# Attention and a gated feed-forward layer on one core: products of zeros between TensorE's early instructions, and a new order of the first two blocks

## The chip, the cores and the metric

The kernel runs on one core of one Trainium2 chip. The time is the device time of one execution in microseconds (us), of which the median of three runs is given. A profile comes from one further execution, whose own time is given beside it.

## The reference

Inputs are q, k, v of shape (4, 8, 768, 64), eight memory keys and values for each head, and the weights of a gated feed-forward layer with 512 inputs and 1536 hidden columns. All is in float32.

```python
for c in range(24):                       # chunks of 32 queries
    q_c   = q[:, :, 32*c : 32*c+32]
    k_ctx = k[:, :, max(0, 32*c-16) : min(768, 32*c+40)]      # 16 to the left, 8 to the right
    k_full = concatenate([mem_k, k_ctx]); v_full = concatenate([mem_v, v_ctx])
    a = softmax(q_c @ k_full.T / 8)
    attn[:, :, chunk] = a @ v_full
x  = attn as (3072 tokens, 512)
xn = x / sqrt(mean(x*x) + 1e-6) * rms_g
g  = xn @ w_gate
out = (g * sigmoid(g) * (xn @ w_val)) @ w_out
```

## The kernel before

The 3072 tokens are worked in eight blocks of 384. A block's attention is four units, each of two heads: unit 0 to 3 belong to block 0, 4 to 7 to block 1. The feed-forward layer goes over twelve slices of 128 hidden columns. Each product of the layer is split into three, of high and low parts, so one slice's gate (or value) is 12 matmuls of 384 columns, and its share of the output is 9 matmuls of 512 columns.

The first two blocks (all of their attention, and most of their feed-forward layer) are issued in the order of a written table, `ORDER`. A token is a letter (the step) and a number (the unit, or a place in the list of slices). Each step issues its instructions on whatever engines it uses, and each engine and each DMA queue works its own instructions strictly in the order of the table. The steps are:

- `U`, `V`: SyncE issues the loads of a unit's q and k, and of its v. `Z`: it issues the load of the next weight chunk.
- `S`: 24 small score matmuls (`s`). `M`, `a`: VectorE takes the row maximum and subtracts it. `E`: ScalarE takes the exponential. `d`, `n`: VectorE sums, inverts and scales.
- `P`: three transposes on TensorE (`pT`). `C`, `m`: ScalarE copies the two halves of the result to SBUF (`pt`). `O`: 12 matmuls with v (`o`).
- `Q`, `G`: ScalarE squares (`xq`), TensorE sums over partitions with a one-column operand (`ss`). `y`: VectorE and GpSimd make the inverse root of the mean. `Y`: TensorE spreads it over the partitions (`rb`, three matmuls). `z`: ScalarE copies it.
- `B`, `D`: ScalarE writes the high part (`xh`), VectorE the low part (`xl`) of the normalised input.
- `p`, `q`: a quarter (three matmuls) of the gate or value of the first slice (`pg`, `pv`). `g`, `v`: a whole gate or value (12 matmuls). `r`, `h`, `i`, `j`, `k`, `l`: what VectorE and ScalarE do on them. `o`: the output matmuls (`po`).
- `J`, `F`, `f`, `I`, `H`, `L`: the steps of ScalarE and VectorE that split a loaded weight chunk into its high and low part.

`p0` to `p3` and `q0` to `q3` are the first slice of block 0, `g1` and `v1` the first of block 1. `Y1` (the second `rb`) stands right behind `v1` in the table of both kernels, and behind it comes `o0`.

Scores, transposes and some other results share three PSUM buffers; gate and value have one bank each, so the next gate waits until VectorE's step `r` has read the last one. At the start, before the table, two matmuls of 512 columns are issued into a bank called `warm` (line 552). A step `W` exists (`warm`, line 187), but the table before has no such token. Behind the table the rest of the kernel (six blocks) is put in order by a scheduler.

Of the kernel before, what the change touches and what calls it, by code (L numbers as in the profile page):

```python
# [9 lines left out]
F32R = mybir.dt.float32r  # L10
# [8 lines left out]
B, H, S, D = 4, 8, 768, 64  # L19
# [5 lines left out]
P = 128  # L25
# [46 lines left out]


ORDER = """
U0 U1 U2 Z U3 S0 U4 M0 a0 U5 S1 M1 a1 V0 S2 E1 E0 M2 d0 J Z V1 U6 S3 a2 n0 E2 M3 P0 V2 F S4 Z C0a a3 m0a n1 E3
V3 f P1 d1 C1a V5 O0 m1a S5 Q0 V4 M4 J n2 U7 O1 a4 B0 n3 E4 G0 M5 B1 V7 I P2 Q1 S6 a5 C2a Z D0 m2a G1 H D1 P3
E5 M6 O2 m3a L C3a d2 O3 Q2 B2 p0 Q3 a6 B3 G2 n5 J G3 n4 F P5 y0 P4 m5a f p1 C5a D2 C4a S7 m4a I E6 O5 M7 Z H
D3 p2 V6 B5 a7 Y0 L E7 O4 d3 z0 Q5 q0 Q4 B4 p3 D5 J q1 n6 q2 n7 P6 D4 P7 f G4 m6a F G5 C6a r0 m7a F O6 C7a h0
I O7 Q6 i0 Z f q3 Q7 B7 G6 B6 D7 G7 J y1 D6 g1 j0 I k0a v1 H l0 Z H F L Y1 L o0 z1 r1 f h1 J g2 I i1 Z H r2 fa
g3 L j1 F v2 k1a l1 I h2 J o1 i2 Z j2 f H v3 r3 k2a F J L g4 l2 I h3 J o2 i3 Z j3 r4 F k3a v4 l3 f h4 fa g5 F  # L80
i4 I H o3 r5 Z j4 I k4a v5 Z H l4 L H g6 L h5 J i5 j5 o4 f J L v6 r6 k5a F J l5 f g7 I h6 fa i6 o5 Z r7 F j6 H
g8 F I k6a L Z H v7 l6 I h7 o6 i7 Z H j7 L k7a v8 J l7 r8 L o7 h8 J i8 f g9 j8 F k8a J I v9 r9 Z l8 f h9 o8 fa
F i9 j9 g10 F k9a I H l9 v10 Z H r10 L J I o9 h10 i10 Z f g11 j10 L k10a J l10 v11 F H r11 I h11 L Z J o10 Z
i11 j11 f k11a g12 H fa v12 J r12 l11 F J F F o11 L h12 I fa Z i12 j12 H g13 F k12a I fa L l12 J v13 I r13 Z H
I L H Z g14 h13 fa i13 L H o12 r14 j13 L k13a v14 J l13 F I h14 F o13 Z H J L F g15 i14 j14 f k14a I v15 r15 H
l14 f h15 J I R0 o14 i15 H L j15 g16 f k15a l15 L v16 r16 F h16 I i16 H o15 L j16
"""


# [1 line left out]
def tile_kernel(ctx: ExitStack, tc: tile.TileContext, q, k, v, w_gate, w_val, w_out, rms_g, out):  # L91
    nc = tc.nc
    const = ctx.enter_context(tc.tile_pool(name="const", bufs=1))
    p1 = ctx.enter_context(tc.tile_pool(name="p1", bufs=1))
    p2 = ctx.enter_context(tc.tile_pool(name="p2", bufs=2))
    p3 = ctx.enter_context(tc.tile_pool(name="p3", bufs=3))
# [37 lines left out]
    def psum_m(tag, name):  # L134
        return psm.tile([P, 512], F32, name=name, tag=tag)
# [49 lines left out]
        return nc.vector.tensor_copy(out=out, in_=in_)  # L185

    def warm(n):

        if ("part", "v", 0) in sp and len(pmw) == 1:
            pmw.append(psum_m("o0", "warm1"))  # L190
        w = pmw[-1]
        for _ in range(n):
            nc.tensor.matmul(w[0:64, 0:64], lhsT=zero, rhs=zero, start=True, stop=True)

    def stage_s(u):
        d = st[u]
# [81 lines left out]
    def stage_p(u, tag=None):  # L278
        d = st[u]
        t = psum_m(tag, f"pT{u}") if tag else psum_a(f"pT{u}")  # L280
        pe = d["p"].rearrange("p j k -> p (j k)")
        for i in range(NT):
            on_pe(nc.tensor.transpose(out=t[:, i * P:(i + 1) * P], in_=pe[:, i * P:(i + 1) * P], identity=ident))  # L283
        d["t"] = t
# [164 lines left out]
    def w_next(fn, *e):  # L449

        c = wpos[fn]
        wpos[fn] += 1
        fn(c, *e)
# [81 lines left out]
    pmw, sp = [], {}  # L535
    manual = tc.manual_schedule()
    manual.__enter__()
    zero = early.tile([P, 64], F32, name="zero", tag="zero")
# [157 lines left out]
    def tok_o(n):  # L696
# [5 lines left out]
    steps = dict(  # L702

        U=load_qk, V=load_v, Z=lambda n: w_load(), W=warm, R=tok_R,

        S=stage_s, M=stage_ma, a=stage_mb, E=stage_e, d=lambda k: stage_da(2 * k), n=stage_db,
        P=lambda n: stage_p(n, "o0" if n < NG else None),
# [7 lines left out]
        J=lambda n: w_next(w_open), F=lambda n: w_next(w_clamp), f=lambda n, *e: w_next(w_sign, *e),  # L715
        I=lambda n: w_next(w_shift),
        H=lambda n, *e: w_next(w_high, *e), L=lambda n, *e: w_next(w_low, *e))
# [638 lines left out]
```

## Time and profile before

| what | value |
|---|---|
| median of three runs | 666.61 us (665.45 to 666.87) |
| the profiled execution's own time | 671.41 us |
| its span, first to last instruction | 669.6 us |
| TensorE busy | 657.9 us (98%) |
| VectorE, ScalarE busy | 503.3 us, 334.7 us |
| mean granted TensorE clock | 0.987 of 2.4 GHz |

A granted clock of 1.00 is 2.4 GHz, 0.50 is 1.2 GHz. PE is TensorE's matmuls, PEld its weight loads, DVE is VectorE, ACT ScalarE, POOL GpSimd, SP the SyncE queue. A matmul's duration in a row holds its way through the array, so rows overlap; what one costs in a dense stretch is the distance from its start to the next start.

### The profile page before, as it was taken

To read this page: it belongs to the slowest core of one execution; us is meant where nothing else is said; L and a number is where in the kernel's file an instruction comes from. 1 tells how busy PE (TensorE), PEld (TensorE's weight loads), DVE (VectorE), ACT (ScalarE), POOL (GpSimd) and SP (SyncE) were. 2 spreads that over 40 slices of the span, in tenths; PEclk is the share of its full clock that TensorE was granted. 3 is DMA by queue.
4 is the path that set the end of the run, shared out by engine and by line. 5 is a ranking of instruction groups with operands and counts; after the bars stand their busy time and mean duration, and the time that the engine had idled before them with its cause. 6 is when DMAs were issued, how large, how long until landed. Compare 5 with 4: busy or idle time off the path is not lost.

```text
span 669.6 us, 15527 instructions
## 1 busy us (share of the span) xinstructions
PE 657.9 (98%) x6238; PEld 612.1 (91%) x6238; DVE 503.3 (75%) x1020; ACT 334.7 (50%) x642; POOL 4.7 (1%) x12
## 2 busy tenths in 40 slices
PE   6999999999999999999999999999999999999998
PEld 4898999999899999989999999999888899999997
DVE  6699999777688788877859567569638378888964
ACT  4779887843434435354445454345335233434553
POOL 0010000000000000000000000000000000000000
PEclk8699999999999999999999999999999999999999
DMA  9645454249698778345439779797643599987102
GB/s 324 251 159 181 185 189 146 106 135 351 187 374 302 254 247 291 107 168 165 143 126 369 262 235 308 253 294 256 191 142 116 170 352 331 320 303 265 52 9 71
DMA packets 82039, 145.46 MB, mean 217 GB/s; under 512 B 7472, under 2 KB 34608, under 8 KB 81968
## 3 DMA queue, kind: packets, MB, share of 16 engines
q1 hardware_dynamic: 80096, 141.32, 62.2%
q10 hardware_dynamic: 1872, 3.15, 1.4%
q8 instruction: 49, 0.80, 0.5%
q14 instruction: 22, 0.18, 0.1%
HBM read 109.84 MB, written 34.60 MB: 216 GB/s over the span
## 4 chain that ended last, share of the span: by engine, by line
PE 88%; DVE 4%; DMA 3%; ACT 2%; issue 1%; SPq 0%; DVEq 0%
PE pg L473 14%; PE po L523 14%; PE pv L473 13%; PE po L1195 8%; PE mva L949 7%; PE mga L949 7%; PE pa L1115 4%; PE mve L949 3%; PE mge L949 3%; PE pe L1115 2%; PE s L220 2%; PE oe L314 2%; PE mgc L949 2%; PE mvc L949 2%; PE pT L283 1%; DMA kv<-qp 1%
## 5 line engine op out<-in xcount | busy, mean ns | idle before, releaser
L473 PE MATMUL pg<-xh,wh_g 128*128 128x384 f32 x192 | 67.3, 351 | 0.7 <-DVE rg L482 0.7
L473 PE MATMUL pg<-xh,wl_g 128*128 128x384 f32 x192 | 65.3, 340 | 0.0
L473 PE MATMUL pg<-xl,wh_g 128*128 128x384 f32 x192 | 65.2, 340 | 0.0
L473 PE MATMUL pv<-xh,wh_v 128*128 128x384 f32 x192 | 65.2, 339 | 0.0
L473 PE MATMUL pv<-xl,wh_v 128*128 128x384 f32 x192 | 64.9, 338 | 0.0
L473 PE MATMUL pv<-xh,wl_v 128*128 128x384 f32 x192 | 64.8, 338 | 0.0
L949 PE MATMUL mva<-x,r 128*128 128x384 f32 x288 | 58.2, 337 | 0.1
L949 PE MATMUL mga<-x,r 128*128 128x384 f32 x288 | 58.2, 337 | 0.1
L523 PE MATMUL po<-wh_o,hh 128*128 128x512 f32 x141 | 56.7, 402 | 0.0
L523 PE MATMUL po<-wl_o,hh 128*128 128x512 f32 x141 | 55.7, 395 | 0.0
L523 PE MATMUL po<-wh_o,hl 128*128 128x512 f32 x141 | 55.7, 395 | 0.0
L949 PEld LDWEIGHTS mga<-x,r 128*128 128x128 f32 x288 | 50.5, 188 | 0.8 <-ACT spare L921 0.4
L949 PEld LDWEIGHTS mva<-x,r 128*128 128x128 f32 x288 | 50.6, 188 | 0.5 <-DVE h L932 0.4
L182 ACT CAST hh<-t 128x384 fp32r<-128x384 f32 x45 | 23.2, 515 | 49.4 <-PE po L523 32.9
L1195 PE MATMUL po<-r,hhs 128*128 128x512 f32 x144 | 45.5, 397 | 0.0
L473 PEld LDWEIGHTS pg<-xh,wh_g 128*128 128x128 f32 x192 | 36.4, 189 | 3.3 <-DVE rg L482 1.0
L473 PEld LDWEIGHTS pg<-xl,wh_g 128*128 128x128 f32 x192 | 36.5, 190 | 1.3
L473 PEld LDWEIGHTS pv<-xh,wh_v 128*128 128x128 f32 x192 | 36.0, 188 | 0.4
L473 PEld LDWEIGHTS pg<-xh,wl_g 128*128 128x128 f32 x192 | 36.3, 189 | 0.0
L473 PEld LDWEIGHTS pv<-xl,wh_v 128*128 128x128 f32 x192 | 36.1, 188 | 0.3
L473 PEld LDWEIGHTS pv<-xh,wl_v 128*128 128x128 f32 x192 | 36.0, 188 | 0.0
L494 DVE TENSOR_TENSOR t<-t,pv 128x384 f32<-128x384 f32 x48 | 26.4, 550 | 10.7 <-PE pv L473 9.5
(252 smaller groups left out, 1600.2 us busy)
## 6 DMA issues: line engine op xcount, KB each, us to landing
r<-kg SPq DMA_DIRECT2D x84, 256.0 KB, 4.9
r<-kv SPq DMA_DIRECT2D x84, 256.0 KB, 4.4
r<-ko SPq DMA_DIRECT2D x68, 256.0 KB, 3.9
kv<-in_v_dram SPq DMA_DIRECT2D x24, 384.0 KB, 4.8
kv<-in_k_dram SPq DMA_DIRECT2D x24, 312.0 KB, 4.1
ws<-in_moe_w_gate_dram SPq DMA_DIRECT2D x4, 1024.0 KB, 4.8
ws<-in_moe_w_val_dram SPq DMA_DIRECT2D x4, 1024.0 KB, 4.8
ws<-in_moe_w_out_dram SPq DMA_DIRECT2D x4, 1024.0 KB, 4.9
```

The lines of the kernel that those rows point to most:

```text
L182: return nc.scalar.copy(out, in_)
L220: on_pe(nc.tensor.matmul(d["s"][a:a + CH, o:o + KC], lhsT=d["q"][r, c * CH:c * CH + CH], rhs=d["k"][r, c // 2, 40 * cp:40 * cp + KC], star ...
L283: on_pe(nc.tensor.transpose(out=t[:, i * P:(i + 1) * P], in_=pe[:, i * P:(i + 1) * P], identity=ident))
L314: on_pe(nc.tensor.matmul(o2[cp][64 * hh:64 * hh + 64, o:o + CH], lhsT=st[u]["v"][r, j, hh], rhs=pt[r, j, hh ^ u % 2], start=True, stop=True))
L473: on_pe(nc.tensor.matmul(ps[:, 0:HT], lhsT=weight(a, n, f, kt), rhs=xs[c][:, kt], start=kt == 0 and i == 0, stop=kt == NKT - 1 and i == 2))
L494: nc.vector.tensor_tensor(out=t, in0=t, in1=vv, op=ALU.mult)
L523: on_pe(nc.tensor.matmul(po[i], lhsT=h[a][:, i * P:(i + 1) * P], rhs=weight(c, "o", f), start=f == first and n == 0, stop=f == end and n = ...
L949: on_pe(nc.tensor.matmul(bank[w, b], lhsT=r[:, a, kt], rhs=x[:, c, kt], start=bool(first) and kt == 0 and i == 0, stop=kt == 1 and i == 2, ...
L1115: on_pe(nc.tensor.matmul(bank[c][i], lhsT=uhl[u][x][:, i * P:(i + 1) * P], rhs=w[y], start=p == 0 and n == 0 and m in (1, 2, 5), stop=p == ...
L1195: on_pe(nc.tensor.matmul(po[i], lhsT=cur[a][:, i * P:(i + 1) * P], rhs=r[c], start=f == n == 0, stop=f == NF - 1 and n == 2))
```

## The change

The step `W` becomes a matmul of a 128x128 stationary operand of zeros with a moving operand of 512 columns of zeros, both read from one column of a zeroed tile, in the one-pass 32-bit format, into the bank `warm`. The table has 21 tokens `W1`, each one such matmul; nobody reads the result. The two matmuls ahead of the table stay. The table is another one in its whole length: the tokens of the two blocks are the same but for `W1`, in another order, for all engines and for the SyncE queue. Behind the table TensorE's, VectorE's, ScalarE's and SyncE's instructions come in the same order as before.

```diff
 ORDER = """
-U0 U1 U2 Z U3 S0 U4 M0 a0 U5 S1 M1 a1 V0 S2 E1 E0 M2 d0 J Z V1 U6 S3 a2 n0 E2 M3 P0 V2 F S4 Z C0a a3 m0a n1 E3
+U0 U1 W1 W1 U2 U3 U4 S0 Z M0 U5 S1 W1 M1 a0 a1 E0 Z S2 E1 V0 d0 V1 S3 V4 M2 Z S4 M3 n0 W1 a2 P0 J V3 W1 a3 W1
...
     def warm(n):
-
-        if ("part", "v", 0) in sp and len(pmw) == 1:
-            pmw.append(psum_m("o0", "warm1"))
-        w = pmw[-1]
+        z = zero[:, 0:1].bitcast(F32R)
         for _ in range(n):
-            nc.tensor.matmul(w[0:64, 0:64], lhsT=zero, rhs=zero, start=True, stop=True)
+            nc.tensor.matmul(pmw[0], lhsT=z.broadcast_to([P, P]), rhs=z.broadcast_to([P, 512]), start=True, stop=True)
```

On TensorE, from unit 2's scores to unit 1's second product, the kernel before has (the number behind a name's first letters is the unit, the one behind the underscore a buffer):

```order
L204 MATMUL s2_221<-k2_145,q2_144 32x64 x24
L204 MATMUL s3_266<-k3_151,q3_150 32x64 x24
L283 MATMUL pT0_297<-ident_102,pe0_185 128x128 x3
L204 MATMUL s4_304<-k4_180,q4_179 32x64 x24
L283 MATMUL pT1_339<-ident_102,pe0_185 128x128 x3
L300 MATMUL o0_351<-pt0_108,vw0_219 64x64 x12
L204 MATMUL s5_365<-k5_188,q5_187 32x64 x24
L300 MATMUL o1_403<-pt1_109,vw1_260 64x64 x12
```

and the changed kernel, at the same place on TensorE:

```order
L202 MATMUL s2_225<-k2_147,q2_146 32x64 x24
L202 MATMUL s3_260<-k3_151,q3_150 32x64 x24
L202 MATMUL s4_291<-k4_155,q4_154 32x64 x24
L191 MATMUL warm_127<-zero_112 128x512
L281 MATMUL pT0_322<-ident_102,pe0_219 128x128 x3
L191 MATMUL warm_127<-zero_112 128x512 x4
L281 MATMUL pT1_350<-ident_102,pe0_219 128x128 x3
L191 MATMUL warm_127<-zero_112 128x512
L202 MATMUL s5_357<-k5_188,q5_187 32x64 x24
L191 MATMUL warm_127<-zero_112 128x512 x2
L298 MATMUL o0_394<-pt0_108,vw0_251 64x64 x12
L298 MATMUL o1_415<-pt1_109,vw1_258 64x64 x12
```

Unit 4's scores stand ahead of unit 0's transposes now, unit 5's ahead of unit 0's second product, and eight products of zeros lie between. Three more stand farther up: two ahead of unit 0's scores and one behind unit 1's.

On TensorE, behind that, from unit 2's transposes to unit 5's, the kernel before has:

```order
L283 MATMUL pT2_431<-ident_102,pe2_291 128x128 x3
L204 MATMUL s6_436<-k6_263,q6_262 32x64 x24
L635 MATMUL ss0_421<-onef_104,xq_135 128x1 x3
L283 MATMUL pT3_472<-ident_102,pe2_291 128x128 x3
L300 MATMUL o2_479<-pt0_108,vw2_301 64x64 x12
L300 MATMUL o3_500<-pt1_109,vw3_336 64x64 x12
L473 MATMUL pg_515<-xh0_130,wh_g0_84 128x384
L473 MATMUL pg_515<-xl0_131,wh_g0_84 128x384
L473 MATMUL pg_515<-xh0_130,wl_g0_85 128x384
L635 MATMUL ss0_421<-onef_104,xq_135 128x1 x6
L283 MATMUL pT5_535<-ident_102,pe4_416 128x128 x3
```

and the changed kernel, from behind unit 1's second product:

```order
L191 MATMUL warm_127<-zero_112 128x512 x2
L281 MATMUL pT2_437<-ident_102,pe2_320 128x128 x3
L633 MATMUL ss0_443<-onef_104,xq_135 128x1 x3
L191 MATMUL warm_127<-zero_112 128x512
L633 MATMUL ss0_443<-onef_104,xq_135 128x1 x3
L191 MATMUL warm_127<-zero_112 128x512 x2
L281 MATMUL pT3_466<-ident_102,pe2_320 128x128 x3
L191 MATMUL warm_127<-zero_112 128x512
L298 MATMUL o2_471<-pt0_108,vw2_334 64x64 x12
L471 MATMUL pg_492<-xh0_130,wh_g0_84 128x384
L471 MATMUL pg_492<-xl0_131,wh_g0_84 128x384
L471 MATMUL pg_492<-xh0_130,wl_g0_85 128x384
```

Unit 6's scores have moved behind unit 3's second product, the first gate quarter has moved ahead of it, and six products of zeros stand in this piece. Four more follow: behind that gate quarter, behind unit 6's scores, and behind unit 6's and unit 7's transposes.

On the SyncE queue, the loads from unit 2 on stand in this order before (`ws` is a weight chunk, `vw` a unit's v):

```order
L162 DMA q2_144<-in_q_dram 128x384
L169 DMA k2_145<-in_k_dram 128x624
L402 DMA ws0_148<-in_moe_w_gate_dram 128x1024
L162 DMA q3_150<-in_q_dram 128x384
L169 DMA k3_151<-in_k_dram 128x624
L162 DMA q4_179<-in_q_dram 128x384
L169 DMA k4_180<-in_k_dram 128x624
L162 DMA q5_187<-in_q_dram 128x384
L169 DMA k5_188<-in_k_dram 128x624
L174 DMA vw0_219<-in_v_dram 128x768
```

and in this one after:

```order
L163 DMA q2_146<-in_q_dram 128x384
L170 DMA k2_147<-in_k_dram 128x624
L163 DMA q3_150<-in_q_dram 128x384
L170 DMA k3_151<-in_k_dram 128x624
L163 DMA q4_154<-in_q_dram 128x384
L170 DMA k4_155<-in_k_dram 128x624
L400 DMA ws0_183<-in_moe_w_gate_dram 128x1024
L163 DMA q5_187<-in_q_dram 128x384
L170 DMA k5_188<-in_k_dram 128x624
L400 DMA ws1_223<-in_moe_w_val_dram 128x1024
L175 DMA vw0_251<-in_v_dram 128x768
```

The first weight chunk goes behind units 3 and 4, and the second one ahead of unit 0's v.

Around the second `rb` (`Y1`) the two tables read, the old one first:

```text
q3 Q7 B7 G6 B6 D7 G7 J y1 D6 g1 j0 I k0a v1 H l0 Z H F L Y1 L o0 z1 r1 f h1 J g2 I
Q7 D6 Z q3 J D7 G6 i0 G7 f g1 H y1 j0 F k0a L J v1 I l0 Z Y1 L o0 z1 H r1 h1 L fa g2
```

Counted from its start, the old table has four tokens `f` and four `I` for VectorE ahead of `r1`, the new one five of each; the fifth ones work a chunk of 1024 columns.

## Rows read from the trace of the kernel before

**Rows 1.** The page: span, and busy time of TensorE and VectorE.

```profile
span 669.6 us, 15527 instructions
PE 657.9 (98%) x6238; PEld 612.1 (91%) x6238; DVE 503.3 (75%) x1020; ACT 334.7 (50%) x642; POOL 4.7 (1%) x12
```

**Rows 2.** Stretches: length, each engine's busy time (instructions), granted clock, DMA share.

```profile
5.07:11.50 6.43, 3.02 (x167) 2.62 (x170) 4.10 (x10) 2.14 (x4) 0.00 (x0) 1.00 1.03 378
11.50:15.00 3.50, 3.35 (x92) 2.64 (x82) 3.37 (x8) 1.98 (x4) 0.00 (x0) 0.51 1.03 401
15.00:21.80 6.80, 5.35 (x159) 4.58 (x160) 6.04 (x14) 5.28 (x13) 0.00 (x0) 1.00 1.04 401
21.80:35.40 13.60, 13.60 (x154) 12.43 (x153) 8.00 (x19) 8.16 (x17) 1.64 (x2) 0.50 0.58 210
35.40:49.60 14.20, 14.14 (x150) 13.68 (x150) 12.68 (x26) 12.69 (x22) 2.04 (x2) 1.00 0.39 129
49.60:65.00 15.40, 14.75 (x80) 13.64 (x80) 14.29 (x20) 13.28 (x15) 0.00 (x0) 1.00 0.56 201
65.00:115.00 50.00, 50.00 (x262) 46.68 (x261) 48.15 (x67) 41.47 (x49) 0.00 (x0) 1.00 0.45 159
```

**Rows 3.** TensorE in order of time: start, duration, instruction, idle before it.

```profile
20.61 0.90 PE L204 MATMUL s<-k,q 64*32 64x64 f32 x48
21.43 1.17 PE L635 MATMUL ss<-onef,xq 128*128 128x1 f32 x6
22.46 0.88 PE L283 MATMUL pT<-ident,pe 128*128 128x128 f32 x3
23.27 2.83 PE L300 MATMUL o<-pt,vw 128*64 128x64 f32 x48
26.03 0.69 PE L473 MATMUL pg<-xh,wh_g 128*128 128x384 f32 x1
...
27.16 2.55 PE L635 MATMUL ss<-onef,xq 128*128 128x1 f32 x12
29.57 1.52 PE L283 MATMUL pT<-ident,pe 128*128 128x128 f32 x6
30.75 0.67 PE L473 MATMUL pg<-xh,wh_g 128*128 128x384 f32 x1
...
31.98 1.52 PE L204 MATMUL s<-k,q 64*32 64x64 f32 x48
33.43 1.55 PE L300 MATMUL o<-pt,vw 128*64 128x64 f32 x24
34.91 0.66 PE L473 MATMUL pg<-xh,wh_g 128*128 128x384 f32 x1
...
39.59 0.82 PE L283 MATMUL pT<-ident,pe 128*128 128x128 f32 x6
40.25 1.40 PE L635 MATMUL ss<-onef,xq 128*128 128x1 f32 x12
41.59 1.90 PE L300 MATMUL o<-pt,vw 128*64 128x64 f32 x48
43.42 0.44 PE L473 MATMUL pv<-xh,wh_v 128*128 128x384 f32 x1
...
44.04 1.39 PE L635 MATMUL ss<-onef,xq 128*128 128x1 f32 x12
...
49.60 0.83 PE L647 MATMUL rb<-ident,srh 128*128 128x128 f32 x6
...
50.51 0.39 PE L523 MATMUL po<-wl_o,hh 128*128 128x512 f32 x1
50.74 0.39 PE L523 MATMUL po<-wh_o,hl 128*128 128x512 f32 x1
```

**Rows 4.** VectorE in order of time: a weight step of 1024 columns.

```profile
46.74 1.22 DVE L436 SCALAR_TENSOR_TENSOR wy<-wy,ws 128x1024 uint32<-128x1024 uint32 x1
```

**Rows 5.** Waits of TensorE between 49.6 and 115 us.

```profile
PE pg L473 <- DVE rg L482: 0.7, 1, 0.7
```

More of the change, by code (lines that the diff above doesn't have):

```diff
@@ L74 @@
 ORDER = """
-U0 U1 U2 Z U3 S0 U4 M0 a0 U5 S1 M1 a1 V0 S2 E1 E0 M2 d0 J Z V1 U6 S3 a2 n0 E2 M3 P0 V2 F S4 Z C0a a3 m0a n1 E3
[L76 to L84, printed above, removed]
@@ L85 @@
-I L H Z g14 h13 fa i13 L H o12 r14 j13 L k13a v14 J l13 F I h14 F o13 Z H J L F g15 i14 j14 f k14a I v15 r15 H
-l14 f h15 J I R0 o14 i15 H L j15 g16 f k15a l15 L v16 r16 F h16 I i16 H o15 L j16
+U0 U1 W1 W1 U2 U3 U4 S0 Z M0 U5 S1 W1 M1 a0 a1 E0 Z S2 E1 V0 d0 V1 S3 V4 M2 Z S4 M3 n0 W1 a2 P0 J V3 W1 a3 W1
+V2 W1 f W1 m0a U6 n1 E2 F C0a I E3 P1 W1 M4 S5 m1a d1 H Z W1 W1 C1a O0 J U7 n2 O1 a4 Q0 M5 W1 B1 W1 F P2 Q1 L
+G0 V5 B0 a5 W1 m2a G1 n3 C2a V6 E4 D0 W1 W1 E5 D1 P3 W1 O2 f m3a C3a d2 p0 B2 W1 J O3 D2 n5 S6 Q2 n4 Q3 W1 B3
@@ new lines @@
+P5 M6 G3 J F a6 G2 I P4 y0 Z S7 f m5a V7 p1 M7 E6 p2 C5a a7 C4a O5 D3 E7 m4a d3 Q5 Y0 B5 O4 H D5 z0 n6 p3 B4
+n7 P6 Q4 W1 D4 P7 m6a W1 f C6a G4 m7a O6 C7a L O7 F B6 I q0 B7 r0 Z G5 Q6 I h0 q1 H q2 Q7 D6 Z q3 J D7 G6 i0
+G7 f g1 H y1 j0 F k0a L J v1 I l0 Z Y1 L o0 z1 H r1 h1 L fa g2 i1 j1 v2 r2 k1a F J l1 I g3 h2 f Z J i2 o1 F j2
+H I v3 k2a Z l2 r3 L h3 g4 J i3 f o2 H r4 j3 F F k3a g5 fa l3 I v4 L Z h4 H i4 I o3 j4 Z H r5 L k4a v5 l4 L h5
+J o4 i5 j5 f J g6 F f k5a v6 J r6 I F Z g7 l5 h6 fa i6 o5 r7 j6 I H v7 F Z k6a L J l6 g8 I h7 H Z i7 o6 j7 H L
@@ L87 @@
+F k7a v8 r8 l7 L h8 o7 i8 j8 f k8a g9 J I Z v9 J F r9 l8 f o8 h9 H i9 j9 g10 F k9a fa l9 I v10 r10 Z L h10 H I
+o9 J i10 Z F f g11 j10 L k10a J l10 v11 f H r11 I h11 o10 i11 Z j11 Z L k11a g12 H l11 J F v12 fa F r12 h12 J
+i12 o11 I J j12 L H F g13 Z I fa F H I v13 fa r13 L k12a J l12 g14 I h13 F Z fa i13 Z L o12 j13 H r14 H I Z
+k13a v14 H l13 L h14 J L o13 f J i14 F j14 L g15 k14a J l14 I F H F v15 f r15 L h15 i15 o14 f j15 I R0 g16 I H
+k15a L H l15 v16 r16 L h16 i16 o15 j16
 """
```

## The prediction, made before the run

> **What bounds the kernel now.** I read the busy times first: TensorE is busy for 98% of the span, VectorE for 75% [rows 1], so a stretch can be shortened there only by removing TensorE's idle time or by making its work quicker. The table of stretches tells where either is to be had [rows 2]. From 5.07 to 21.8 us TensorE is busy 3.02 + 3.35 + 5.35 = 11.7 of 16.7 us. The DMA share is 1.03 to 1.04 all that while, so the loads set the pace, and 5.0 us of TensorE stand empty. From 21.8 to 35.4 it has no idle time, but the granted clock is 0.50: it works at 1.2 GHz. From 35.4 on the clock is 1.00, and up to 115 us TensorE idles 0.06 + 0.65 us; the wait in this is one for VectorE's step `r`, which frees the gate's bank [rows 5].
>
> The same instructions at both levels, by the distance from one start to the next, show that the low clock costs nearly its full factor [rows 3]: six transposes 29.57 to 30.75 = 1.18 us against 39.59 to 40.25 = 0.66; twelve one-column products 2.41 against 1.34 (40.25 to 41.59); a gate quarter 1.13 or 1.23 against 0.62 (43.42 to 44.04); 48 products with v 2.76 against 1.83; one unit's scores 1.45 against 0.82 (20.61 to 21.43). Before the clock fell near 21.8, TensorE had idled 1.45 of 6.8 us [rows 2] and ended on one-column products; during the low stretch it did transposes, one-column products and small products with v, with two short gate quarters. It came back at about 35.4, behind scores and products with v that followed each other closely.
>
> **The low stretch: what there is to win.** From 22.46 to 34.91 us, 12.45 us, stand three transposes, 48 products with v, a gate quarter, twelve one-column products, six transposes, a gate quarter, one unit's scores, 24 products with v [rows 3]. At the full clock they would take 0.33 + 1.83 + 0.62 + 1.34 + 0.66 + 0.62 + 0.82 + 0.92 = 7.14 us: 5.3 less. The whole 13.6 us at the same ratio give 5.8 us. There is another low stretch, 11.5 to 15 us. I cost it at nothing: the loads set the pace there, and a quicker TensorE would only wait longer for them; without that cover it would be worth up to half of 3.35 us.
>
> **The 21 products.** No row shows a product of zeros; the nearest is an output product of 512 columns in the same format, which costs 50.74 - 50.51 = 0.23 us at the full clock [rows 3], and about 0.42 us at the half clock by the ratio of the gate quarter, 1.13 / 0.62. All 21 cost 4.8 us at the full clock. Sixteen of them stand ahead of unit 3's transposes, where the kernel before is at about 22 us: 3.7 us against 5.0 us of empty time. I cost these at nothing, as the loads are still late there; without that cover they cost the 3.7. The other five cost 5 x 0.23 = 1.2 us, and I charge them in full, because TensorE has no idle time there. So TensorE by itself allows 5.8 - 1.2 = 4.6 us.
>
> **The loads and the order.** With the first weight chunk behind units 3 and 4, their scores can run earlier, and unit 0's v comes one weight chunk later. The chunk is the size of a unit's q and k, and from 5 to 21.8 us the queue is full, so both shifts are of the order of a third of the 5.0 us of empty time, in opposite directions. The same bytes are loaded by the time TensorE has all its data. I take both orders as level at 21.8 us; by how much the new one is ahead or behind no row tells. A shift by one unit's scores either way would be 0.8 us.
>
> **VectorE and ScalarE: what comes late instead.** A quicker TensorE runs into steps of the other engines: transposes wait for `n`, products with v for the copies `m`, `Y0` for `y`. The common point of both orders is `Y1`, at 49.60 us [rows 3]. From 21.8 to there VectorE is busy 8.00 + 12.68 = 20.7 us of 27.8 [rows 2]. The new table has one token `f` and one `I` more ahead of `r1`, each 1.22 us on a 1024-column chunk like the row shown [rows 4], so 23.1 us of work. At the share at which VectorE runs in the full-clock stretch, 12.68 / 14.20 = 89%, this takes 25.9 us; at its best share, 48.15 / 50.00 = 96% [rows 2], it takes 24.0. So VectorE lets `Y1` come 1.9 to 3.8 us earlier, less than TensorE's 4.6. I take the middle, 2.8 us. The two added steps don't have to be done later, so I expect VectorE to keep pace behind `Y1`; from there to 115 us TensorE is the full one, and beyond that the order of the engines is unchanged, so that the 2.8 us reach the end.
>
> **The sum.** 671.41 - 2.8 = 668.6 us for a profiled execution. The median of the runs is 4.8 us below the profiled one, and I take the difference over: 666.6 - 2.8 = 663.8 us.
>
> **Rivals.** *All of it comes back:* VectorE isn't the limit because its work is spread better, and the one wait of 0.65 us [rows 5] goes as well: 4.6 + 0.65 = 5.2 us, 661.4 us. For it speaks that VectorE's idle time in the low stretch was waiting for a slow TensorE; against it that VectorE has more to do before `r1`.
>
> *Given back behind `Y1`:* TensorE arrives early, but VectorE and ScalarE, 93% and 86% busy from 49.6 to 65 us and 96% and 83% from 65 to 115 us [rows 2], come no earlier with the weights and the steps `r` to `l`, and new waits for `r` eat the gain. VectorE's free time from 49.6 to 115 is 1.1 + 1.85 = 3.0 us, which could absorb some 2.3 of the 2.8: 666.1 us.
>
> *The low clock isn't there to win in the timed runs:* the profiled execution is 4.8 us above the median, close to the 5.8 us that the low stretch costs it. If the runs without the profiler don't have this stretch, the products can win nothing and are hidden at best: 666.6 us, within half a us. Against it: the three runs agree within 1.4 us, and the profiler can cost this much in other ways.
>
> *The clock falls all the same (slower):* the place is the one-column sums and transposes of units 2 and 3, behind `o1`. The products ahead of it have then been spent, and the ten behind it run at the half clock, 10 x 0.42 = 4.2 us, against TensorE's idle time of 1.45 us from 15 to 21.8 [rows 2]. With the low stretch as long as before this is 2.8 us slower, 669.4 us. It decides from the point at which more than about two thirds of the low stretch stays, since then 5.8 us x a third no longer pay for the products. For it speaks that the clock had also fallen at 11.5 us, behind a stretch with scores in it [rows 2]; against it that the products lie in just the places where TensorE was empty. The Trainium skill has a rule that bears on this, in "TensorE: Matmul & The Clock Gate", Part 1, "What's actually happening": how many products run cold at a kernel's start differs from run to run, since the clock's monitor does not start with the kernel, and one shouldn't fit to a count. By that rule an order that holds the clock in one execution may lose it in another, and this rival's time would be met in some of them; a single profile of before can't show it.
>
> **How the numbers follow.** Forecast (about 2.8 us faster, its own range 662 to 665.2) 0.50; all of it back 0.08; given back 0.14; nothing there to win 0.13; clock falls 0.15. A difference under 0.2%, 1.3 us, is one that a measurement here can't tell from none. Faster by more: 0.46 of the forecast, 0.08, and 0.05 of the next two, together 0.59. Slower by more: the 0.15, less 0.02 in which it is small, plus 0.03 for late loads, 0.16. The same: the rest, 0.25. The range runs from 660.7, just under the case in which all comes back, to 668.6, which takes in the hidden cases and the milder part of the fallen clock.
>
> **What would show it.** Right, if the granted clock is 1.00 from about 15 us to the end but for one short dip at most; if TensorE's second `rb` starts near 47 us; if VectorE is over 90% busy from 22 us to there; and if the stretch behind it, to the end, is as long as before within half a us. The idle time ahead of unit 3's transposes should be under 3 us, with the products of zeros about 0.23 us apart where several stand together. Wrong, if the clock is at 0.50 for over 8 us behind 15 us (the slower rival), if the second `rb` is early but TensorE has over 2 us of new waits between it and 115 us (given back), or if the profile is shorter by 3 us or more while the median is not (nothing there to win).

## The result, and the profile after: slower by about 1.2%

The changed kernel takes 675.94 us, median of six runs (671.42 to 676.74), the one before 666.33 us, median of six on the same chip. The ratio over all runs is 1.0115 with a 95% interval of 1.0081 to 1.0149; the medians alone lie 9.6 us, 1.4%, apart, because the six runs fall into two groups: two of 671.4 and 672.6 us at a mean granted clock of 0.995, four of 675.7 to 676.7 us at 0.990 to 0.992. A second series, of 6 runs on another occasion (e9 below), gave 676.17 us and 1.013 (1.0096 to 1.0164). The forecast was 663.8 us.

The profiled execution took 671.42 us, the same as the one profiled before (671.41 us). So the two profiles together don't show the loss; but they differ in what fills the time. First the page of the changed kernel, span and busy times [rows 1]:

```profile
span 669.5 us, 15575 instructions
...
PE 658.6 (98%) x6259; PEld 611.3 (91%) x6259; DVE 503.3 (75%) x1020; ACT 334.0 (50%) x642; POOL 4.1 (1%) x12
```

Then its stretches, with the same columns as [rows 2]: length, busy time of PE, PEld, DVE, ACT and POOL, granted clock, DMA share, GB/s.

```profile
5.07:11.50 6.43, 5.38 (x216) 3.98 (x216) 3.55 (x9) 0.99 (x2) 0.00 (x0) 1.00 1.03 382
11.50:15.00 3.50, 1.72 (x30) 1.37 (x30) 3.50 (x8) 1.24 (x2) 0.00 (x0) 0.64 1.03 404
15.00:21.80 6.80, 6.64 (x98) 4.90 (x97) 5.03 (x12) 5.04 (x10) 0.00 (x0) 0.68 1.04 403
21.80:35.40 13.60, 12.02 (x212) 10.40 (x212) 9.95 (x23) 11.10 (x23) 1.49 (x2) 1.00 0.50 177
35.40:49.60 14.20, 13.88 (x166) 13.16 (x167) 13.70 (x25) 13.15 (x24) 1.58 (x2) 1.00 0.58 215
```

The low stretch from 21.8 to 35.4 us is gone: the clock is 1.00 (2.4 GHz) there, against 0.50 (1.2 GHz) [rows 2]. It is low earlier instead: 0.64 and 0.68 in the two stretches from 11.5 to 21.8 us, against 0.51 and 1.00. And yet TensorE in order of time is late (start, duration, instruction, idle before it):

```profile
10.86 0.53 PE L202 MATMUL s<-k,q 64*32 64x64 f32 x20 [0.27 <-DMA k<-in_k_dram]
13.28 1.08 PE L202 MATMUL s<-k,q 64*32 64x64 f32 x28 [1.90 <-issue]
14.29 0.79 PE L191 MATMUL warm<-zero 128*128 128x512 f32 x1
14.88 0.85 PE L281 MATMUL pT<-ident,pe 128*128 128x128 f32 x3
15.38 2.06 PE L191 MATMUL warm<-zero 128*128 128x512 f32 x4
17.32 0.90 PE L281 MATMUL pT<-ident,pe 128*128 128x128 f32 x3
...
20.38 1.27 PE L298 MATMUL o<-pt,vw 128*64 128x64 f32 x36
23.38 0.57 PE L298 MATMUL o<-pt,vw 128*64 128x64 f32 x12 [1.74 <-issue]
...
24.42 0.49 PE L281 MATMUL pT<-ident,pe 128*128 128x128 f32 x3
...
50.88 0.83 PE L645 MATMUL rb<-ident,srh 128*128 128x128 f32 x6
```

Two things are to be seen. Unit 4's scores break off behind their 20th record and go on 1.90 us later, and unit 1's product with v breaks off in its middle for 1.74 us. The profile names no releaser for either gap ("issue"): it shows no other engine and no load that ends one. And the second `rb` starts at 50.88 us, 1.3 us later than before [rows 3], although a stretch at half the clock has been won back. From there to the end it is 669.5 - 50.9 = 618.6 us against 620.0, and the wait for step `r` [rows 5] no longer stands. In another profile of the changed kernel (e9) it is 672.3 - 52.6 = 619.7 us, so one profile gives this part to about 1 us only.

### The profile page after: what moved, and what is told of

Its sections match the earlier page's. It is cut to its first block, busy times and chain, and to the rows that moved or that the text cites. A ratio compares the mean times of both kernels' runs of the same rounds, so it can differ in the third digit from the quotient of the medians.

```text
span 669.5 us, 15575 instructions
## 1 busy us (share of the span) xinstructions
PE 658.6 (98%) x6259; PEld 611.3 (91%) x6259; DVE 503.3 (75%) x1020; ACT 334.0 (50%) x642; POOL 4.1 (1%) x12
## 4 chain that ended last, share of the span: by engine, by line
PE 94%; DVE 2%; DMA 1%; issue 1%; ACT 1%; SPq 1%
PE po L521 15%; PE pg L471 15%; PE pv L471 15%; PE po L1193 8%; PE mva L947 8%; PE mga L947 7%; PE pa L1113 4%; PE mve L947 4%; PE mge L947 4%; PE oe L312 2%; PE s L218 2%; PE mgc L947 2%; PE pe L1113 2%; PE pT L281 2%; PE mvc L947 2%; PE pc L1113 1%
## 5 line engine op out<-in xcount | busy, mean ns | idle before, releaser
L501 DVE TENSOR_TENSOR hl<-t,hh 128x384 fp32r<-128x384 f32 x45 | 24.9, 553 | 12.4 <-ACT hh L183 12.2
```

The source lines that it names most:

```text
L501: nc.vector.tensor_tensor(out=hl, in0=t, in1=hh.bitcast(F32), op=ALU.subtract)
```

## The experiments

In "time", the median in us, with the lowest and highest run; "ratio" is against the kernel before on the same chip, with its 95% interval. "2nd rb" is the start of the second `rb` in that kernel's profile, "idle" is TensorE's idle time from 5.07 us to there, both in us.

| kernel | order of loads | order on engines | products | time | ratio | 2nd rb | idle |
|---|---|---|---|---|---|---|---|
| e1 | old | old | 0 | 666.5 (665.8 to 672.7) | 1.001 (0.999 to 1.003) | 44.46 | 4.6 |
| e12 | old | old | 16 | 667.4 (666.8 to 669.5) | 1.0005 (0.999 to 1.002) | 45.88 | 3.8 |
| e3 | old | old | 21 | 670.4 (668.0 to 675.3) | 1.006 (1.004 to 1.008) | 46.64 | 3.6 |
| e10 | old | new | 0 | 672.8 (672.4 to 673.2) | 1.008 (1.005 to 1.011) | 52.15 | 8.8 |
| e5 | old | new | 21 | 670.9 (669.7 to 677.7) | 1.009 (1.006 to 1.012) | 48.76 | 5.8 |
| e6 | new | old | 0 | 673.2 (671.3 to 674.9) | 1.009 (1.006 to 1.013) | 52.35 | 6.1 |
| e2 | new | new | 0 | 673.8 (673.2 to 674.0) | 1.010 (1.008 to 1.012) | 52.65 | 9.5 |
| e8 | new | new | 11 | 674.9 (674.5 to 675.8) | 1.012 (1.009 to 1.016) | 52.39 | 5.7 |
| e9, the changed kernel | new | new | 21 | 676.2 (672.6 to 678.8) | 1.013 (1.010 to 1.016) | 52.56 | 6.0 |
| e4 | new | new, ten small matmuls ahead | 21 | 671.4 (670.4 to 672.6) | 1.007 (1.005 to 1.009) | 49.54 | 3.8 |
| e7 | old up to the second `rb`, then new | the same | 0 | 667.4 (666.5 to 669.4) | 1.001 (0.999 to 1.003) | 45.13 | 4.3 |
| e11 | new, one chunk later | new, its weight steps later | 21 | 674.6 (670.5 to 677.7) | 1.010 (1.007 to 1.014) | 50.78 | 4.6 |

In the profile of the changed kernel that the last section shows, the idle time is 4.9 us.

**e1: the kernel before once more.** No edit.

> The kernel before, unchanged, to see the granted clock and span of its timed runs. If its profiled execution (671.4 us at a mean clock of 0.987) was an untypical one, with more of the low clock than the timed runs, their mean clock is 0.992 or more at spans of 664 to 666 us. If the profiler itself costs the 4.8 us, their clock is 0.987 as well.

Its mean clock was 0.994 to 0.999 in ten of twelve runs (665.8 to 669.2 us), and 0.987 in two, which took 671.9 and 672.7 us. Its profiled execution is one of the ten, at 666.25 us. Its stretches:

```profile
5.07:11.50 6.43, 4.38 (x166) 3.60 (x169) 3.66 (x7) 2.00 (x4) 0.00 (x0) 0.97 1.03 375
11.50:15.00 3.50, 2.97 (x90) 2.33 (x81) 3.43 (x10) 1.55 (x5) 0.00 (x0) 0.56 1.03 403
15.00:21.80 6.80, 5.13 (x162) 4.36 (x156) 6.07 (x14) 5.34 (x12) 0.00 (x0) 1.00 1.03 399
21.80:35.40 13.60, 13.24 (x217) 12.11 (x207) 12.25 (x28) 12.96 (x25) 1.65 (x2) 1.00 0.71 266
35.40:49.60 14.20, 14.10 (x125) 13.21 (x125) 13.20 (x22) 11.79 (x20) 2.04 (x2) 1.00 0.44 149
```

The stretch from 21.8 to 35.4 us runs at 1.00, with the kernel unchanged. TensorE, in order of time:

```profile
11.03 1.50 PE L204 MATMUL s<-k,q 64*32 64x64 f32 x48 [1.80 <-DMA k<-in_k_dram]
...
13.87 1.21 PE L204 MATMUL s<-k,q 64*32 64x64 f32 x48
...
19.88 0.83 PE L635 MATMUL ss<-onef,xq 128*128 128x1 f32 x6 [0.94 <-issue]
20.57 0.53 PE L283 MATMUL pT<-ident,pe 128*128 128x128 f32 x3
...
44.46 0.83 PE L647 MATMUL rb<-ident,srh 128*128 128x128 f32 x6
```

So the execution that was profiled before was one of the few with the low stretch; an ordinary run has nothing of that kind to win. Measured against this one, the changed kernel's profile is 6.4 us late at the second `rb` (50.88 against 44.46), and 3.9 us already at unit 2's transposes (24.42 against 20.57).

What the 6.4 us consist of can be read from the stretches of the two profiles. From 5.07 to 49.6 us TensorE's idle time, length less busy time, is 4.9 us in the changed kernel and 4.7 us here: the products have not made it shorter. Busy time times the missing part of the clock is 1.72 x 0.36 + 6.64 x 0.32 = 2.7 us there and 4.38 x 0.03 + 2.97 x 0.44 = 1.4 us here. The 21 products at 0.23 us are 4.8 us of new work. Together that is 0.2 + 1.3 + 4.8 = 6.3 us, an estimate, as a half clock does not cost each instruction its full factor.

**e2: the new table without its products.**

```diff
-U0 U1 W1 W1 U2 U3 U4 S0 Z M0 U5 S1 W1 M1 ...     (21 tokens W1)
+U0 U1 U2 U3 U4 S0 Z M0 U5 S1 M1 ...
```

> The new table without its 21 products of zeros. If the loss comes from the new order (TensorE's gaps of 1.9 and 1.7 us inside unit 4's scores and unit 1's product with v), those two gaps stay, at the same instructions counted from the start less those of the products, and the time is 672 us or more. If the products are what costs (4.8 us at the full clock, more at the half clock), the time falls to 666 to 668 us.

673.8 us: the order alone is slower by 1.0%, most of what the whole change costs. Its stretches:

```profile
5.07:11.50 6.43, 3.95 (x216) 3.42 (x216) 3.59 (x9) 0.98 (x2) 0.00 (x0) 1.00 1.01 357
11.50:15.00 3.50, 1.30 (x37) 0.84 (x29) 3.38 (x8) 1.85 (x4) 0.00 (x0) 0.97 1.03 408
15.00:21.80 6.80, 5.10 (x98) 4.42 (x99) 6.27 (x14) 4.49 (x9) 0.00 (x0) 0.51 1.03 400
21.80:35.40 13.60, 10.84 (x187) 9.15 (x187) 7.94 (x18) 11.13 (x21) 1.49 (x2) 0.87 0.55 205
35.40:49.60 14.20, 13.86 (x159) 12.76 (x158) 12.53 (x24) 11.57 (x21) 0.20 (x1) 0.88 0.40 150
```

TensorE is idle for 9.5 us from 5.07 to 49.6 us, twice as long as in e1. The products of the changed kernel fill that idle time again, to 4.9 us, but are 4.8 us of work themselves. The gaps stay, 1.54 and 1.06 us; the first now stands behind the 23rd record of unit 4's scores, three later than with the three products that stood ahead of it, the second behind the 47th record of the two products with v, eleven later, which is the number of products that went. The mean clock is 0.987 to 0.990 in all four runs, lower than before. Without products the new order doesn't hold the clock. With them the time is no better: 1.010 (1.008 to 1.012) without, 1.012 (1.008 to 1.015) and 1.013 (1.010 to 1.016) with.

**e3 and e12: products in the old table.** e3 puts 21 `W1` into the old table, e12 the first 16 of them:

```diff
+ W1: 2 behind U1, 1 S1, 3 S2, 1 P0, 2 P1, 2 S5, 2 O1, 1 G0, 2 G1                  (both)
+ W1: 1 behind each of P3, p0, G3, p1, p2                                          (e3 alone)
```

> The old table with 21 products of zeros put into TensorE's early waits (behind units 1's and 2's scores, the transposes, unit 5's scores, unit 1's product with v, the one-column sums). If the order is what costs, the clock holds better than before and the time is 662 to 666 us. If the products cost, or bring the gaps by being more instructions, it is 668 to 675 us, with gaps of over 1 us inside a step of small matmuls.

> The old table with 16 products in TensorE's early waits, those of e3 ahead of unit 3's transposes. The prediction had such products at nothing. If they are, this kernel runs at 666 to 667 us and e3's other five cost the rest. If they push TensorE's work back although it has empty time, 668.5 to 670 us, of e3's 670.4.

Sixteen cost nothing that can be told from none (1.0005, 0.999 to 1.002), and the mean clock was 0.994 or more in all ten runs. The stretches of e12:

```profile
5.07:11.50 6.43, 5.06 (x176) 3.63 (x179) 3.86 (x8) 2.04 (x4) 0.00 (x0) 1.00 1.02 374
11.50:15.00 3.50, 2.45 (x94) 1.96 (x85) 3.47 (x9) 2.00 (x4) 0.00 (x0) 1.00 1.04 402
15.00:21.80 6.80, 5.65 (x113) 4.41 (x112) 5.85 (x14) 4.38 (x9) 0.00 (x0) 1.00 1.03 400
21.80:35.40 13.60, 13.33 (x250) 12.01 (x248) 10.96 (x26) 12.12 (x25) 1.64 (x2) 1.00 0.69 252
```

The clock is 1.00 throughout, and yet nothing is won. The products have not vanished in empty time either: up to 35.4 us TensorE is idle for 3.8 us against 4.6 us in e1, 0.8 us less for 3.7 us of products, and the clock gives back the 1.4 us that e1 loses. The second `rb` is 1.4 us later than in e1 (45.88 against 44.46), of which the whole span keeps 0.5 us (665.0 against 664.5). The other five cost 670.4 - 667.4 = 3.0 us where I had put 1.2; the two kernels ran on different chips, and by the ratios it is 0.5%, 3.5 us. In the profiles 0.8 us of it stands ahead of the second `rb` (46.64 against 45.88); behind it e3 takes 668.0 - 46.6 = 621.4 us, e12 665.0 - 45.9 = 619.1. e3's waits of TensorE behind 45 us show part of the difference; the one of 0.8 us for VectorE is not in e12:

```profile
PE pg L470 <- DVE t L488: 0.8, 1, 0.8
PE pg L470 <- DVE rg L479: 0.6, 1, 0.6
```

Whether five products ahead of 33 us are the cause of waits behind 45 us stays open.

**e4: ten more small matmuls ahead of the table.**

```diff
+    zz = zero[:, 0:1].bitcast(F32R)
+    for _ in range(10):
+        nc.tensor.matmul(pmw[0][:, 0:8], lhsT=zz.broadcast_to([P, P]), rhs=zz.broadcast_to([P, 8]), start=True, stop=True)
```

> The changed kernel with 10 more matmuls (8 columns of zeros) ahead of the table, where TensorE still waits for its first load. If the two gaps inside a step stand at a fixed count of TensorE's instructions (a block of them that has not arrived), each moves 10 matmul records earlier: the first from behind the 20th record of unit 4's scores to behind the 10th, the second from behind the 36th record of the two products with v to behind the 26th. If they are waits for data, a bank or the clock, they stay behind the same records. The time changes by less than 2 us.

TensorE in order of time:

```profile
11.28 0.41 PE L202 MATMUL s<-k,q 64*32 64x64 f32 x10 [0.27 <-DMA k<-in_k_dram]
13.86 0.83 PE L202 MATMUL s<-k,q 64*32 64x64 f32 x38 [2.17 <-issue]
...
19.95 1.03 PE L298 MATMUL o<-pt,vw 128*64 128x64 f32 x26
21.77 0.86 PE L298 MATMUL o<-pt,vw 128*64 128x64 f32 x22 [0.79 <-issue]
```

The first gap moves from behind the 20th record to behind the 10th, the second from behind the 36th to behind the 26th: they stand at a fixed count of TensorE's instructions. Each record is a weight load and a matmul, and from one gap to the next in the changed kernel the records, those left out above among them, are 28 + 1 + 3 + 4 + 3 + 1 + 48 + 2 + 36 = 126, or 252 instructions. The page's table of DMA queues has a queue for instructions, and in the stretches of half a us in which its first two packets run, it shows, for the changed kernel (packets, MB, share of 16 engines; 10.5 to 11 us, then 20.5 to 21 us):

```profile
q8 instruction: 49, 0.80, 0.5%
...
q8 instruction: 1, 0.02, 12.6%
...
q8 instruction: 1, 0.02, 13.3%
```

Forty-nine packets of 0.80 MB are 16 KB each, and 2 x 6259 instructions of TensorE by 49 are 255. So TensorE waits for the next block of its instructions: it goes on at 13.28 and 23.38 us, each 2.3 to 2.9 us behind the start of a packet. The DMA share is 1.03 from 10.5 to 13.3 us and 1.04 from 20.5 to 23.4 us. In e9 the first packet runs from 12.5 us on, two us later, and TensorE goes on at 14.98 us:

```profile
11.56 0.53 PE L202 MATMUL s<-k,q 64*32 64x64 f32 x20 [0.26 <-DMA k<-in_k_dram]
14.98 1.08 PE L202 MATMUL s<-k,q 64*32 64x64 f32 x28 [2.89 <-issue]
```

The Trainium skill, "Runtime: NRT & Kernel Launch", section "Instruction fetch mechanics", says that instructions come in 16 KiB blocks of 256, fetched by a queue of the sequencer's own, and that crossing a block's end is mostly hidden. The trace agrees on the block, and with 49 blocks and two such gaps of over 1 us behind 5 us in the changed kernel also on "mostly"; those two cost 1.9 and 1.7 us, in e9 2.9 and 1.8. In the old order the count of the first gap is reached in unit 4's scores at 13.87 us, after their block (its packet is at 11 us in e1's trace), because unit 3's scores wait 1.80 us for a load ahead of it; the new order has brought the scores forward into the time in which the block is still under way. The second block's end delays the old order as well: the first gap of the changed kernel stands behind 215 records from the table's start, the second behind 341, and e1's 0.94 us before its sums of 19.88 us and a gap in e12 behind 342:

```profile
18.03 0.59 PE L297 MATMUL o<-pt,vw 128*64 128x64 f32 x13
19.72 0.56 PE L297 MATMUL o<-pt,vw 128*64 128x64 f32 x11 [1.10 <-issue]
```

e3 has the same gap with 0.97 us, not quite the 1 us that was expected for it. The time of e4, 671.4 us, is 4.6 and 4.8 us lower than the changed kernel's in its two series, with the clock at 0.996 or more in all four runs; less than 2 us had been expected. Why ten small matmuls at the start keep the clock up stays open.

**e5 and e10: the new table with the loads in the old order**, with and without products; **e6: the old table with the loads in the new order.** The first 21 tokens `U`, `V` and `Z` of the one table are put into the places of those of the other:

```diff
-U0 U1 U2 U3 U4 Z U5 Z V0 V1 V4 Z V3 V2 U6 Z U7 V5 V6 Z V7
+U0 U1 U2 Z U3 U4 U5 V0 Z V1 U6 V2 Z V3 V5 V4 U7 V7 Z Z V6        (e5, e10; the reverse in e6)
```

> The new table with its 21 products, but with the loads on the SyncE queue in the old order (the first 21 load tokens). If the new order of loads is what costs, by bringing unit 0's v late and by letting TensorE run into a block of instructions that isn't there yet, the gap in unit 4's scores shrinks under 1 us, the second rb starts 2 to 4 us earlier than in the changed kernel, and the time is 667 to 669 us. If the order on the engines and the products cost, the time stays at 671 us or more.

> The new table without products and with the loads in the old order; what is left of the change is the order on the engines. If the order on the engines costs by itself, the second rb starts 2 us or more later than at 44.5 us and the time is 668.5 us or more. If in e5 (670.9 us) the products cost all of the 4.5 us, this kernel is at 666 to 667.5 us.

> The old table without products, with the loads in the new order. If the order of the loads costs by itself, the second rb starts 2 us or more later than at 44.5 us and the time is 668 to 670 us. If not, 665.5 to 667.5 us.

In e5 both gaps are gone, and the clock is 1.00 from 5 to 65 us in its profile. The time is 670.9 us all the same: six of ten runs at a mean clock of 0.994 to 0.999 took 669.7 to 671.2 us, four at 0.990 to 0.992 took 674.5 to 677.7 us. Its second `rb` is at 48.76 us, 2.9 us behind e12's. In its stretches

```profile
5.07:11.50 6.43, 4.12 (x154) 2.88 (x157) 3.49 (x9) 2.20 (x4) 0.00 (x0) 1.00 1.02 358
11.50:15.00 3.50, 2.55 (x102) 2.25 (x102) 3.04 (x7) 0.08 (x1) 0.00 (x0) 1.00 1.04 405
15.00:21.80 6.80, 6.08 (x118) 4.82 (x117) 6.63 (x15) 6.35 (x13) 0.00 (x0) 1.00 1.03 399
21.80:35.40 13.60, 12.22 (x238) 10.52 (x239) 10.70 (x25) 11.74 (x23) 1.49 (x2) 1.00 0.75 271
35.40:49.60 14.20, 13.72 (x136) 13.21 (x133) 13.93 (x22) 11.99 (x20) 1.58 (x2) 1.00 0.49 154
```

TensorE is idle for 1.4 + 0.5 = 1.9 us between 21.8 and 49.6 us, e12 for 0.3 us; from 5.07 us on it is 5.8 us, so with the gaps gone TensorE waits elsewhere, 3.3 us of it for loads of k. Without products (e10) the clock falls, 0.986 to 0.990 in all four runs, TensorE is idle for 8.8 us, and the time is 672.8 us: the order on the engines costs by itself, as one of the two expectations had it (668.5 us or more), and e5's products make no difference in the ratio that the intervals can tell (1.009 against 1.008). e6 also costs 1%, more than the 668 to 670 us expected: its mean clock is 0.982 to 0.990. Neither e10 nor e6 has a gap at a block's end. ScalarE's waits up to 40 us in e6 show what the new order of loads does to it:

```profile
ACT pt L181 <- PE pT L282: 5.2, 4, 2.3
ACT ws L416 <- DMA ws<-in_moe_w_gate_dram: 3.0, 1, 3.0
```

The second line is not in e1's trace: ScalarE stands for 3.0 us at the first weight chunk, which the new order loads behind units 3 and 4, with exponentials and copies queued behind it. Part of it reaches TensorE: VectorE stands 1.31 us for ScalarE's step on that chunk, and TensorE's transposes at 15.91 us wait 1.75 us for VectorE's step queued behind it. The changed kernel has the same wait of ScalarE with 3.1 us.

**e11: the weight steps later.** In the new table `J f F I H` of the first chunk are moved behind `C1a`, and the load that reuses the chunk's buffer behind `V6`:

```diff
-... P0 J V3 W1 ... V2 W1 f W1 ... F C0a I E3 ... m1a d1 H Z W1 W1 C1a O0 ... V6 E4 ...
+... P0 V3 W1 ... V2 W1 W1 ... C0a E3 ... m1a d1 W1 W1 C1a J f F I H O0 ... V6 Z E4 ...
```

> The changed kernel with the first weight chunk's steps on ScalarE and VectorE moved behind unit 1's copies (and the load that reuses its buffer behind unit 6's v). In the changed kernel ScalarE waits 3.1 us for that chunk, with unit 0's copies and the next exponentials queued behind it. If this wait is part of the loss, it is gone, the second transposes and unit 0's product with v come 1 to 3 us earlier, and the time is 1 to 3 us under that of the changed kernel. If the missing block of instructions or the loads hold TensorE anyway, the time stays within 1 us of it, or grows, as the first gate quarter comes later.

ScalarE's wait is gone, both gaps stay (1.62 and 1.98 us), the second `rb` is at 50.78 us, and the time is 674.6 us (670.5 to 677.7, five runs), which overlaps with e9's 672.6 to 678.8. It doesn't tell whether that wait was part of the loss.

**e8: the first eleven products alone.** The ten `W1` behind `O0` are taken out of the new table.

> The new table with only the first 11 products, those ahead of unit 0's product with v. If the ten behind cost their price on TensorE's path, 10 times 0.23 us, and are not needed for the clock, the time is 2 us under that of the changed kernel on the same chip (e4's 671.4 as a guide: 669). If they hold the clock, the granted clock falls again between 20 and 35 us and the time is 672 us or more.

674.9 us, at a mean clock of 0.989 to 0.992. Its stretches show where the clock goes, 0.75 from 21.8 to 35.4 us, and gaps of 2.6 us each in place of 1.90 and 1.74. As far as one profile of each shows, the ten products hold the clock there, as one of the two expectations had it; the time is level with the changed kernel's.

**e9: the changed kernel once more.** No edit.

> The changed kernel, unchanged, beside the three others on one chip. If its two levels, 671 to 672 us and 676 to 677 us, are the clock's doing, the runs at a mean clock of 0.995 and more stay near 671 and those at 0.992 and less near 675 to 677. If they are the chip's, all runs lie within 1.5 us of each other.

Two runs at a mean clock of 0.995 took 672.6 and 674.2 us, four at 0.990 took 675.3 to 678.8. The clock parts the runs, as expected, though the first two lie above the 671 us that had been named; and even the best is 6 us above the kernel before, so the lower clock of most runs is not the whole loss.

**e7: the old table up to the second `rb`, the new one behind it**, without products.

> The old table up to the second rb, without products, then the rest of the new table. In the profiles the time from the second rb to the end is 618.6 us in the changed kernel against 620.0 in the one before, where TensorE also waits 0.65 us for step r. If this is the order behind the second rb, this kernel is 0.5 to 1.5 us faster than before (665 to 666 us). If it comes only from work that the new table does ahead of it, the time is 666 to 668 us.

667.4 us (1.0008, 0.999 to 1.003): no gain. So the order behind the second `rb` wins nothing; the 1.4 us that one profile of the changed kernel shows there (0.3 us in e9's) are not its doing. No kernel in this study is faster than the one before.

## Why the prediction was wrong, point by point

**The loads and the order** is the step that failed with the largest price: "I take both orders as level at 21.8 us". By its own words no row told it, and it was put at nothing. The order alone, without a product, costs 1.0% by the ratio (e2), 6.6 us of 666.3; the half of it on the engines costs 0.8% (e10), the half on the load queue 0.9% (e6). At 21.8 us the changed kernel is behind: unit 2's transposes come 3.9 us later than in an ordinary run of before. What the runs show in place of "level" is TensorE's idle time ahead of the second `rb`, 9.5 us in e2 and 8.8 in e10 against 4.6 in e1, and a mean clock of 0.982 to 0.990 in all twelve runs of e2, e10 and e6, against 0.994 or more in most runs of before. The ends of the instruction blocks are one part of this, and not the main one: the two gaps are 3.6 us, the old order has 0.9 us of the same, and e10 and e6, with one half of the new order each, have no gap and still lose 0.8 and 0.9%. That ScalarE's wait for the first weight chunk is the main reason in e6 is only argued.

**The low stretch: what there is to win** is the second. "From 22.46 to 34.91 us ... 5.3 less. The whole 13.6 us at the same ratio give 5.8 us" was right of the execution profiled, and was then carried over to the median by taking over the difference of 4.8 us. That difference was the low stretch: e1's ordinary run has the clock at 1.00 there and a span of 664.5 us, so the 2.8 us that the forecast takes off were not there to be won. Of what I gave a chance of 0.13, that the stretch isn't there in the timed runs, the first half was true; that the products would then be "hidden at best" fits the time of sixteen in the old table (e12), not the change. "Nearly its full factor" was too much for the products with v, which went from 1.83 to 2.76 us, a factor of 1.5 against 1.8 for the other rows.

**The 21 products.** "Sixteen ... at nothing" came out in the old table (e12), but not for the reason given. They were to vanish in 5.0 us of empty time, and 0.8 us of it went; the clock and the part behind the second `rb` paid for the rest. In the new order they filled idle time that the order itself had made, and bought back no time (e2 against e9, e10 against e5). Five at 1.2 us was not right in the old table: about 3 us, of which 0.8 stands ahead of the second `rb`.

**VectorE and ScalarE.** TensorE's wait for VectorE in the stretch from 21.8 us to `Y1` was 0.33 us in the profile after, so VectorE was not what set the pace there; it was busy for 23.65 of 27.8 us, 85%, not over 90%. The wait for `r` went, and the time behind `Y1` fell by 1.4 us in one profile and 0.3 us in another, where I had expected half a us at most.

**The clock falls all the same** was the rival on the slower side, 0.15. Its time, 669.4 us, lies on the side of what happened, its place does not: the ten products after `o1` ran at the full clock in the profile after, and the low stretch lay at 12 to 19 us, beside the first gap. In the timed runs the mean clock of the changed kernel is 0.990 to 0.995, in the first series and in e9, against 0.994 or more in most of before. A mean of 0.990 in place of 0.997 is 674 x 0.007 = 4.7 us, an estimate that fits the 4 us between the two groups of runs; where in those runs the clock falls no profile shows.

So of the 12.1 us between the forecast of 663.8 us and the measured median, 2.5 lead back to the time of before, as there was no low stretch to win, and 6.6 are the order (e2). The remaining 3 us of the medians come with the products; by the ratios it is 1 to 2 us, which the intervals don't tell from none. e3 and e5 both lose about 4 us at the higher clock, but not in one place: in the profiles e5 is 4.3 us late at the second `rb` (48.76 against 44.46) and 3.8 us at the end, e3 2.2 and 3.5 us. So e3 does not show what the products cost in the new order. What stays open is why each half of the order costs nearly as much as the whole, why the clock falls in some runs of one kernel and not in others, and why a block of instructions is asked for when it is.

## What to carry to other kernels

Before a stretch of one profile is counted as winnable, look whether the timed runs have it: where a profiled execution is slower than all the runs shown, and it holds a low clock that costs about that difference, it is likely an untypical one, and one more profile settles it. Where small matmuls are brought forward on TensorE into a time in which the loads fill the queue, look at the count of its instructions as well as at its data: the next block of them may still be under way. A new order is a term with a price of its own: run it without what it was made for. And products put into empty time are work: look whether the idle time has become shorter by as much.

## What the runs showed of the hardware

TensorE stopped for up to 2.9 us inside a step of small matmuls, at a fixed count of its instructions, some 250 apart, and went on 2 to 3 us behind the start of a 16 KB packet on the instruction queue. Such gaps are listed as "issue", as the profile shows nothing that ends them. The mean granted clock of one and the same kernel, on one chip, lay between 0.987 and 0.999 in twelve runs, and its time between 665.8 and 672.7 us with it.
